# Whole float32 weights for the first token block of an attention and two-layer MLP kernel

## The chip, the cores and the metric

The kernel runs on one core of a Trainium2 chip. The metric is the device time of one execution in microseconds (us); the median of three runs of the kernel before is 1067.43 us (1066.63 to 1068.05).

## What is computed

```python
scores = scale * np.matmul(q, k.transpose(0, 1, 3, 2))     # q, k, v: (4, 8, 576, 64)
thresh = np.max(scores, axis=-1, keepdims=True) - tau
scores = np.where(scores >= thresh, scores, -1000000000.0)
attn = softmax(scores)
x = (attn @ v) as 2304 tokens x 512
h = x @ w_in;  x = where(h > 0, h, exp(min(h, 0)) - 1) @ w_out      # first layer, 512 -> 2048 -> 512
h = x @ w_in2; out = maximum(0.01 * h, h) @ w_out2                  # second layer
```

All inputs are float32, but the weights arrive as float64 words, which the kernel turns into float32 itself.

## The kernel before

Attention is cut into 32 groups: 8 ranges of queries (4 or 5 units of 64 queries) times 4 pairs of heads. A group loads `in` (K and Q, L417) and `v` (L419). For each unit TensorE makes the scores s (L446); VectorE moves them to ss with their extreme value (L450) and makes the threshold (L456); ScalarE cuts (L461) and takes the exponential (L464); VectorE inverts the sum (L467); GpSimd multiplies e by it (L469). The result has to be turned. In the first four groups TensorE turns it against an identity matrix into the PSUM tile y (L484), and two copies a unit (512 and 128 columns, L313 on ScalarE or L314 on VectorE) bring it to p. In the others VectorE transposes 32x32 blocks into t (L489), and 16 DMAs a group (L539, 13 from SP and 3 from GpSimd) exchange the blocks to p. Then TensorE multiplies p by v (L553) and a copy writes x.

Beside attention run seven blocks of 256 tokens of the first layer, each over the first 8 of 16 slices f of the hidden dimension (L591: h = x @ w_in slice; L603 to L610: g; L634: y += g @ w_out slice). To reach float32 accuracy at the rate of the reduced type fp32r, each operand is split into a rounded part (xh, wih, gh) and the rest (xl, wil, gl), and each product is three passes: high by high, low by high, high by low (`passes`, L575). The 16 tiles of weights (8 slices, wi and wo) go through `weight` (L316): DMA to wraw (L321), the high words scaled to wa (L327), the low words shifted to wb (L331, L333), two merges with two operands on VectorE (L338, L341), then rounding to wih or woh (L306, L308, L309) and a subtraction for wil or wol (L302, L303). From about 428 us attention is over, and the rest of the first layer and the second run in blocks of 512 tokens.

The order on every engine is not written out. `Order.run` (L114) is a planner: each operation has engines it may run on, a cost, what it depends on and a due time `vt`; the planner walks a modelled clock and on each engine takes the ready operation that is due first. The numbers in `KN`, the costs (`POOLI`, `LAND`, `ISSUE` and so on) and the letters that name the allowed engines (`ka='A'`: ScalarE) set the order, which is then fixed in each engine's queue. SP's queue too is in order: a DMA whose buffer is not free keeps back the ones behind it.

Of the kernel before, what the change touches and what calls it, by code (L numbers as in the profile page):

```python
# [38 lines left out]
POOLI = 1000  # L39
# [8 lines left out]
    pad=18, stay=2646.41, late=1.3, margin=0, look=0.00348273, warm=3, tu=2231.35, lead=15280.3, wv0=-1642.63,  # L48
    wv1=-1629.68, early=2925.04, boff=18361.1, bdt=7113.64, yoff=1471.44, coff=-454.38, wb=140.292, w2a=2637.92,
    o1=-3645.43, o2=1772.81, o3=4927.53, o4=-3359.29, o5=4040.73, o6=-25.7749, mo=4440.99, ka='A', kl='PA', kh='AD',  # L50
    ko='D', kt='D', kx='AD', kxl='DP', km='DP', kg='PA', kgl='P', kgl1='D', kd='DP', kc='AD', kn='P', kv='A')
# [178 lines left out]
LAND = 2100.0  # L230
ISSUE = 450
# [25 lines left out]
def attn_moe_kernel(ctx, tc, kqv, tau, w1i, w1o, w2i, w2o, yp, out):  # L257
# [21 lines left out]
    wb_r = ring(stg, 1, [128, 512], F32, "wb_")  # L279
# [36 lines left out]
    def weight(layer, which, f, vt, after=(), reg=False):  # L316
        raw, a, b = raw_r.new(), wa_r.new(), wb_r.new()
        hi, lo = wdst[which, f, "h"].new(), wdst[which, f, "l"].new()
# [24 lines left out]
            op0=ALU.bitwise_and, op1=ALU.bitwise_or), PORT), [ob], [raw, b], vt)  # L343
        oh = op(hi_of(KN["kh"], 512, hi, b), [ob], [b, hi], vt)
# [60 lines left out]
    ld = op(sp(128, 4, lambda: nc.sync.dma_start(out=taut, in_=tau.partition_broadcast(128))), [], [], -9e5)  # L405
# [4 lines left out]
    def group(gi, p, vts):  # L410
# [9 lines left out]
            out=v().rearrange("p h c d -> p (h c d)"), in_=kqv[gi * NE + p][:, KQV - 10 * D:KQV])), [], [v], due + 8e3)  # L420
# [14 lines left out]
        def units(js, vt):  # L435
# [56 lines left out]
            elif gi < GP:  # L492
                for z in range(m):
# [7 lines left out]
                    copies(lambda t=t: t()[:, 0], t, o, 0, 4, z)  # L501
                    copies(lambda t=t: t()[:, 1, 0:128], t, o, 4, 5, z)
# [26 lines left out]
    def values(gi, p, n, w, vt, by_pe, turned, tg, pg, v, lv, blocks):  # L529
        b, u0, u1 = GROUPS[gi]  # L530
        got = turned
        if not by_pe:
            got = []
            for z, (a, d) in enumerate((a, (a + r) % 4) for r in range(4) for a in range(4)):
# [6 lines left out]
                if z * NG // 16 != (z + 1) * NG // 16:  # L541
                    got.append(op((POOL, POOLI, lambda copy=copy: copy(nc.gpsimd)), turned, [pg, tg], vt + KN["o4"],
                                  lat=2500))
                else:
                    got.append(op(sp(32, 20 * w, lambda copy=copy: copy(nc.sync), 620), turned, [pg, tg],
                                  vt + KN["o4"]))
# [33 lines left out]
    def step_h(layer, f, tb, xc, hps, vt, reg):  # L580
# [14 lines left out]
        for k in range(KC):  # L595
            o = op((PE, 3 * mm(tb), lambda k=k: mms(k)), [o, wi[2], xc[k][2]],
                   [hg, wi[0], wi[1], xc[k][0], xc[k][1]], vt)
# [4 lines left out]
        if layer == 0:  # L602
# [21 lines left out]
    def step_y(layer, f, first, last, tb, g, ybank, ysl, vt):  # L624

        wo = wt[layer, "wo", f]
        res = []
        for m in range(KC):
            yg, share, end = ybank[m]

            def mms(m=m, yg=yg, share=share, end=end):
                cs = slice(m * 128, (m + 1) * 128)
                for z, (w_, g_) in enumerate(passes(wo, g)):
# [4 lines left out]
            res.append(op((PE, 3 * mm(tb), mms), [wo[2], g[2], g[3], *prev],  # L638
                          [yg, wo[0], wo[1], g[0], g[1]], vt))
# [4 lines left out]
    def block(layer, t0, fs, tb, deps, hps, yrings, evac, vt0, dt, reg=False):  # L644
        xc = conv_x(t0, tb, deps, vt0 - dt + (KN["coff"] if reg else 0), reg)
# [184 lines left out]
```

## Time and profile before

| | |
|---|---|
| median of 3 runs | 1067.43 us (1066.63 to 1068.05) |
| the profiled execution: own time, span | 1070.21 us, 1068.4 us |
| TensorE matmuls (PE) busy | 1019.3 us, 95% |
| VectorE (DVE), ScalarE (ACT), GpSimd (POOL) busy | 596.1, 508.2, 264.4 us |
| mean granted TensorE clock | 0.977 |
| DMA traffic | 120.15 MB |

The profile is one execution. Busy time of TensorE counts overlapping matmuls once; the duration of one matmul includes its way through the array, so what a matmul costs in a row of them is the distance of two starts. "PEclk" is the granted clock in parts of full speed. A releaser in brackets is what ended the idle time before an instruction. SPq is SP's queue of DMA issues.

### The profile page before, as it was taken

The page shows a single profiled execution, that of the slowest core. Times are in us where ns is not written, and L with a number is a line of the kernel's source. Part 1 is how long each engine was busy: PE and PEld are TensorE (multiplying, and loading weights), DVE is VectorE, ACT ScalarE, POOL GpSimd, SP SyncE. Part 2 cuts the span into 40 slices and gives each one's busy share as a digit, 9 for nine tenths or more (in the row PEclk, how much of TensorE's full clock was granted, in tenths as well). Part 3 has the DMA queues.
Part 4 walks back from the last instruction along what each step waited for, and adds up shares of the span by engine and source line. Part 5 has one row for each costly group of instructions (what it writes and reads, how often), then busy time and mean ns, then how long its engine had stood idle before and what let it go on. Part 6 is the DMA issues. An engine that isn't in the chain of part 4 may idle for free.

```text
span 1068.4 us, 17123 instructions
## 1 busy us (share of the span) xinstructions
PE 1019.3 (95%) x6294; PEld 807.7 (76%) x6294; DVE 596.1 (56%) x1228; ACT 508.2 (48%) x1027; POOL 264.4 (25%) x411
## 2 busy tenths in 40 slices
PE   7868899998999999999999999999999999999998
PEld 3435667776777777788888889888888888888898
DVE  6797767876777773898986547851311311221221
ACT  6887766767667673554563225532222221222221
POOL 4555655666556564101000000000000000000000
PEclk7878999999999999999999999999999999999999
DMA  6466777778777766435443003310100100010010
GB/s 207 154 181 200 203 198 201 208 210 216 189 214 193 220 184 166 140 118 187 149 124 131 28 13 99 120 60 1 40 0 1 40 1 1 1 40 1 1 40 21
DMA packets 48564, 120.15 MB, mean 112 GB/s; under 512 B 9888, under 2 KB 14496, under 8 KB 48480
## 3 DMA queue, kind: packets, MB, share of 16 engines
q1 hardware_dynamic: 45792, 111.18, 35.8%
q0 software_dynamic: 2688, 7.87, 2.7%
q8 instruction: 50, 0.82, 0.3%
q14 instruction: 34, 0.28, 0.1%
HBM read 67.63 MB, written 9.44 MB: 72 GB/s over the span
## 4 chain that ended last, share of the span: by engine, by line
PE 81%; DMA 6%; SPq 4%; DVE 3%; ACT 2%; issue 2%; POOL 0%; POOLq 0%; ACTq 0%; DVEq 0%
PE y L634 35%; PE h L591 20%; PE hb L591 15%; PE v L553 7%; PE s L446 5%; SPq L539 3%; DMA p<-t 2%; DMA in<-in_kqv_dram 2%; DMA wraw<-in_w1o_dram 1%; DVE t L489 1%; DVE ss L450 1%; PE y L484 1%; DMA wraw<-in_w1i_dram 0%; ACT e L464 0%; ACT p L313 0%
## 5 line engine op out<-in xcount | busy, mean ns | idle before, releaser
L634 PE MATMUL y<-gh,woh 128*128 128x512 f32 (+1 forms) x736 | 255.4, 347 | 2.2 <-ACT ysx L313 1.4
L634 PE MATMUL y<-gl,woh 128*128 128x512 f32 (+1 forms) x736 | 252.0, 342 | 0.0
L634 PE MATMUL y<-gh,wol 128*128 128x512 f32 (+1 forms) x736 | 251.7, 342 | 0.0
L302 DVE TENSOR_TENSOR gl<-g,gh 128x512 fp32r<-128x512 f32 (+1 forms) x128 | 83.6, 654 | 273.2 <-ACT g L617 263.4
L591 PE MATMUL h<-xh,wih 128*128 128x256 f32 (+1 forms) x480 | 163.7, 341 | 15.8 <-ACT g L603 7.2
L634 PEld LDWEIGHTS y<-gh,woh 128*128 128x128 f32 x736 | 138.9, 189 | 31.9 <-issue 10.7
L591 PE MATMUL h<-xl,wih 128*128 128x256 f32 (+1 forms) x480 | 158.2, 330 | 0.5 <-DVE xl L302 0.2
L591 PE MATMUL h<-xh,wil 128*128 128x256 f32 (+1 forms) x480 | 157.7, 329 | 0.0
L634 PEld LDWEIGHTS y<-gl,woh 128*128 128x128 f32 x736 | 139.0, 189 | 16.1
L634 PEld LDWEIGHTS y<-gh,wol 128*128 128x128 f32 x736 | 138.8, 189 | 16.2
L450 DVE TENSOR_SCALAR_CACHE_REDUCE ss<-s,scl 128x576 f32<-128x576 f32 x144 | 114.5, 799 | 31.7 <-PE s L446 31.5
L591 PEld LDWEIGHTS h<-xh,wih 128*128 128x128 f32 x480 | 90.9, 189 | 43.6 <-issue 10.4
L469 POOL TENSOR_SCALAR e<-e,su 128x576 f32<-128x576 f32 x144 | 110.2, 776 | 40.5 <-DVE su L467 35.3
L461 ACT ACTIVATE ss<-ss,thr 128x576 f32<-128x576 f32 x144 | 105.3, 769 | 16.8 <-DVE thr L456 16.4
L464 ACT ACTIVATE e<-ss,taun 128x577 f32<-128x577 f32 x144 | 110.8, 771 | 1.1 <-DVE t L489 0.4
L489 DVE STREAM_TRANSPOSE t<-e 128x640 f32<-128x640 f32 x128 | 102.2, 825 | 13.8 <-POOL e L469 7.1
L446 PE MATMUL s<-in 64*64 64x288 f32 x1152 | 95.5, 443 | 11.3 <-DVE ss L450 7.0
L553 PE MATMUL v<-p,v 128*64 128x320 f32 (+1 forms) x640 | 98.0, 439 | 7.3 <-DMA p<-t 4.3
L591 PEld LDWEIGHTS h<-xl,wih 128*128 128x128 f32 x480 | 91.0, 190 | 9.5 <-DVE xl L302 0.9
L591 PEld LDWEIGHTS h<-xh,wil 128*128 128x128 f32 x480 | 91.1, 190 | 8.2
L591 PE MATMUL hb<-xh,wih 128*128 128x512 f32 (+1 forms) x256 | 94.5, 369 | 0.0
L591 PE MATMUL hb<-xl,wih 128*128 128x512 f32 (+1 forms) x256 | 94.5, 369 | 0.0
(438 smaller groups left out, 1218.4 us busy)
## 6 DMA issues: line engine op xcount, KB each, us to landing
p<-t SPq DMA_DIRECT2D x208, 100.0 KB, 3.1
p<-t SPq DMA_DIRECT2D x156, 80.0 KB, 3.3
v<-in_kqv_dram SPq DMA_DIRECT2D x32, 320.0 KB, 3.9
in<-in_kqv_dram SPq DMA_DIRECT2D x16, 608.0 KB, 4.5
in<-in_kqv_dram SPq DMA_DIRECT2D x16, 544.0 KB, 4.3
wraw<-in_w1i_dram SPq DMA_DIRECT2D x16, 512.0 KB, 3.8
wraw<-in_w1o_dram SPq DMA_DIRECT2D x16, 512.0 KB, 3.7
wraw<-in_w2i_dram SPq DMA_DIRECT2D x16, 512.0 KB, 3.5
```

The costliest lines, as they stand in the source:

```text
L302: return pick(who, D=(dve(n), lambda: nc.vector.tensor_tensor(**args()), PORT), P=(pool_tt(n), lambda: nc.gpsimd.tensor_tensor(**args())))
L446: nc.tensor.matmul(s[z]()[64 * h:64 * h + 64, i, 0:HALF], q()[r, at:at + 64], k()[r, h], start=True, stop=True)
L450: om = [op((DVE, dve(S) + 160, lambda z=z: nc.vector.tensor_scalar(out=ss[z]()[:, 0:S].rearrange("p (j c) -> p j c", j=2), in0=s[z]()[:, : ...
L461: o = op((ACT, act(S) + 95, lambda z=z: nc.scalar.activation(out=ss[z]()[:, 0:S], in_=ss[z]()[:, 0:S], func=AF.Prelu, bias=thr()[:, z:z + ...
L464: oe.append(op((ACT, act(S) + 190, lambda z=z: nc.scalar.activation(out=e[z]()[:, 0:S + 1], in_=ss[z]()[:, 0:S + 1], func=AF.Exp, bias=tau ...
L469: on = [op(pick(KN["kn"], P=(pool_ts(S) + 90, lambda z=z: nc.gpsimd.tensor_scalar(out=e[z]()[:, 0:S], in0=e[z]()[:, 0:S], scalar1=su()[:, ...
L484: nc.tensor.transpose(dst, e[z]()[:, c * 128:(c + 1) * 128], ident)
L489: turned.append(op((DVE, dve(SX) + 70, lambda z=z, cols=cols: nc.vector.transpose(out=blocks(tg).rearrange("p d c q -> p c d q")[:, :, :, ...
L539: q.dma_start(out=to[0]()[to[1], to[2]], in_=fr[0]()[fr[1], fr[2]])
L553: nc.tensor.matmul(ps()[64 * h:64 * h + 64, 0:64 * n], v()[:, h, c, :], blocks(pg)[:, 2 * h:2 * h + 2, c], start=(c == 0), stop=(c == 4))
L591: nc.tensor.matmul(hp(), w_()[:, cs], x_()[:, 0:tb], start=(k == 0 and z == 0), stop=(k == KC - 1 and z == 2))
L634: nc.tensor.matmul(ysl(yg, m), w_()[:, cs], g_()[:, 0:tb], start=(first and z == 0 and share == 0), stop=(last and z == 2 and end))
```

## The change

For the first block of 256 tokens (`NATIVE = 1`) the kernel multiplies the merged float32 weights, x and g as they are: `step_h` and `step_y` issue one float32 matmul where three split passes stood, `conv_x` is left out, and g needs no rounding and no subtraction. The merged weights live in 17 slots of their own, so that they stay until block 0 is done; `split_w` makes the high and low parts for the later blocks with due times of their own, the low part being written into a slot whose float32 weight is no longer used. The two copies from y to p become one of 640 columns. Tau's load, the loads of v, and block 0 get due times of their own; costs in the planner and most numbers in `KN` differ, and with them the engines allowed (wa to GpSimd, x copies to VectorE, rounding of weights to GpSimd or ScalarE).

```diff
-POOLI = 1000
+POOLI = 520
+SPI = 690
+NATIVE = 1
...
-    pad=18, stay=2646.41, late=1.3, margin=0, look=0.00348273, warm=3, tu=2231.35, lead=15280.3, wv0=-1642.63,
...
-    ko='D', kt='D', kx='AD', kxl='DP', km='DP', kg='PA', kgl='P', kgl1='D', kd='DP', kc='AD', kn='P', kv='A')
+    pad=18, stay=1957.74, late=1.3, margin=0, look=0.00348273, warm=2, tu=1933.47, lead=15925.1, wv0=975.379,
...
+    o4=-3200.93, o5=4767.88, o6=-29.7579, mo=-5087.01, ka='P', kl='PA', kh='PA', ko='D', kt='D', kx='A', kxl='DP',
+    km='DP', kg='A', kgl='DP', kgl1='D', kd='P', kc='AD', kn='P', kv='D')
...
-LAND = 2100.0
-ISSUE = 450
+LAND = 2500.0
+ISSUE = 500
...
+    slots = [Ring(lambda dt, s=s: stg.tile([128, 512], dt, tag=f"w{s}", name=f"w{s}"), 1) for s in range(2 * FH + 1)]
...
+        n = 2 * f + (which == "wo")
+        raw, a, b = raw_r.new(), wa_r.new(), slots[n if reg else 2 * FH - 1].new(F32)
...
+        wt[layer, which, f] = (b, ob)
+        if not (reg and NATIVE):
+            split_w(layer, which, f, vt, reg)
+
+    def split_w(layer, which, f, vt, reg):
+        b, ob = wt[layer, which, f]
+        n = 2 * f + (which == "wo")
+        hi = wdst[which, f, "h"].new()
+        lo = slots[(n - 1) % (2 * FH + 1)].new(F32R) if f < FH else wdst[which, f, "l"].new()
...
-    ld = op(sp(128, 4, lambda: nc.sync.dma_start(out=taut, in_=tau.partition_broadcast(128))), [], [], -9e5)
+    ld = op(sp(128, 4, lambda: nc.sync.dma_start(out=taut, in_=tau.partition_broadcast(128))), [], [], KN["tl"])
...
-            out=v().rearrange("p h c d -> p (h c d)"), in_=kqv[gi * NE + p][:, KQV - 10 * D:KQV])), [], [v], due + 8e3)
+            out=v().rearrange("p h c d -> p (h c d)"), in_=kqv[gi * NE + p][:, KQV - 10 * D:KQV])), [], [v], due + KN["vl"])
...
-                    copies(lambda t=t: t()[:, 0], t, o, 0, 4, z)
-                    copies(lambda t=t: t()[:, 1, 0:128], t, o, 4, 5, z)
+                    copies(lambda t=t: t().rearrange("p b c -> p (b c)")[:, 0:640], t, o, 0, 5, z)
...
+            if whole:
+                nc.tensor.matmul(hp(), wi[0]()[:, cs], xc[k][1], start=(k == 0), stop=(k == KC - 1))
+                return
...
+                o = op((PE, mm32(tb), lambda k=k: mms(k), True), [o, wi[1], *xc[k][2]], [hg, wi[0]], vt)
...
+            d = gh if whole else g
...
+            if whole:
+                return gh, None, o, o
...
+                    nc.tensor.matmul(ysl(yg, m), wo[0]()[:, cs], g[0]().bitcast(F32)[:, 0:tb],
+                                     start=(first and share == 0), stop=(last and end))
...
+        if reg and t0 < NATIVE * TA:
+            xc = [(None, x[:, k, t0:t0 + tb], deps[k]) for k in range(KC)]
...
+        if i == NATIVE - 1:
+            for f in range(FH):
+                for j, which in enumerate(("wi", "wo")):
+                    split_w(0, which, f, need * TU + KN["wp0"] + (2 * f + j) * KN["wp1"], True)
```

How the order moves, at three places. TensorE, from the fourth value group (v<-p,v) on, before; wih and wil are the parts of the first weight slice, xh and xl those of a quarter of x:

```order
L553 MATMUL v<-p,v 64x256 x10
L446 MATMUL s<-in 64x288 x8
L591 MATMUL h<-xh_731,wih_171 128x256
L591 MATMUL h<-xl_743,wih_171 128x256
L591 MATMUL h<-xh_731,wil_176 128x256
L591 MATMUL h<-xh_368,wih_290 128x256
```

and now, w being a whole weight tile:

```order
L564 MATMUL v<-p,v 64x256 x10
L603 MATMUL h<-x,w_144 128x256
L603 MATMUL h<-x,w_232 128x256
L458 MATMUL s<-in 64x288 x8
L603 MATMUL h<-x,w_232 128x256 x3
L458 MATMUL s<-in 64x288 x12
L603 MATMUL h<-x,w_326 128x256 x4
L656 MATMUL y<-gh,w_197 128x256 x4
```

One row stands where three stood; the place beside the value groups is much the same. GpSimd, its first rows of work on weights and e, before:

```order
L331 TENSOR_SCALAR wb__149<-wraw 128x512
L303 TENSOR_TENSOR wil_176<-wb__149,wih_171 128x512
L331 TENSOR_SCALAR wb__184<-wraw 128x512
L469 TENSOR_SCALAR e_89<-e_89,su 128x576
L469 TENSOR_SCALAR e_90<-e_90,su 128x576
L303 TENSOR_TENSOR wol_246<-wb__184,woh_232 128x512
```

and now:

```order
L328 TENSOR_SCALAR wa__146<-wraw 128x512
L309 TENSOR_SCALAR wih_170<-w_144 128x512
L306 TENSOR_TENSOR w_175<-w_144,wih_170 128x512
L328 TENSOR_SCALAR wa__183<-wraw 128x512
L481 TENSOR_SCALAR e_89<-e_89,su 128x576
L481 TENSOR_SCALAR e_90<-e_90,su 128x576
L309 TENSOR_SCALAR woh_219<-w_197 128x512
```

GpSimd makes wa, which ScalarE made, and rounds weights, which VectorE or ScalarE did; w_175 is a low part. SP, in the middle of attention, before (t_87 and t_88 are the turned groups, `in` and v the loads of later groups):

```order
L539 DMA p<-t_88 32x800 x9
L419 DMA v<-in_kqv_dram 128x640
L539 DMA p<-t_88 32x800 x4
L417 DMA in<-in_kqv_dram 128x1088
L539 DMA p<-t_87 32x640 x8
L419 DMA v<-in_kqv_dram 128x640
L539 DMA p<-t_87 32x640 x5
```

and now:

```order
L550 DMA p<-t_88 32x800 x13
L429 DMA in<-in_kqv_dram 128x1088
L431 DMA v<-in_kqv_dram 128x640
L550 DMA p<-t_87 32x640 x13
L429 DMA in<-in_kqv_dram 128x1088
L431 DMA v<-in_kqv_dram 128x640
```

The load of v stands behind all 13 copies of a group where it stood among them.

## Rows read from the trace of the kernel before

**Rows 1.** Busy by stage: PE, PEld, DVE, ACT, POOL, PEclk, DMA, GB/s
```profile
0.00:145.00 145.00, 114.11 (x854) 70.08 (x856) 110.08 (x257) 107.97 (x227) 76.78 (x110) 0.85 0.63 189
145.00:425.00 280.00, 267.49 (x2359) 199.32 (x2357) 200.78 (x484) 190.01 (x418) 167.03 (x271) 0.99 0.75 200
425.00:1069.00 644.00, 637.73 (x3085) 538.34 (x3081) 285.21 (x489) 210.22 (x382) 20.61 (x30) 1.00 0.18 57
```

**Rows 2.** Chain of waits, 0 to 145 us, shares by line
```profile
by line: PE v L553 15.9%; DMA wraw<-in_w1o_dram 8.8%; issue 7.7%; PE s L446 6.9%; DMA p<-t 6.3%; SPq L539 5.8%; PE y L484 3.7%; DVE t L489 3.2%; PE h L591 2.8%; ACT e L464 2.8%; DVE ss L450 2.6%; ACT p L313 2.2%; DVE wil L302 1.5%; POOL e L
```

**Rows 3.** Groups of instructions, ScalarE, 0 to 145 us: busy us, mean ns
```profile
L313 ACT COPY p<-y 128x128 f32<-128x128 f32 (+1 forms) x20 | 7.4, 409 | 2.4 <-DVE p L314 2.4
L313 ACT COPY x<-v 128x256 f32<-128x256 f32 (+1 forms) x8 | 3.2, 395 | 10.5 <-PE v L553 10.5
L308 ACT ACTIVATE gh<-g 128x256 fp32r<-128x256 f32 x7 | 2.8, 404 | 1.6 <-DVE g L610 1.6
L333 ACT ACTIVATE wb__365<-wraw,lowb 128x512 uint32<-128x512 uint32 x1 | 0.8, 777 | 0.0
L327 ACT ACTIVATE wa__328<-wraw 128x512 f32<-128x512 f32 x1 | 0.7, 670 | 0.0
```

**Rows 4.** The same view, VectorE
```profile
L314 DVE COPY p<-y 128x512 f32<-128x512 f32 (+1 forms) x12 | 6.0, 521 | 6.8 <-PE y L484 5.4 <-ACT p L313 1.4
...
L302 DVE TENSOR_TENSOR wil<-wb__258,wih 128x512 fp32r<-128x512 f32 x1 | 0.7, 693 | 0.4 <-ACT wih L308 0.4
...
L309 DVE TENSOR_SCALAR wih<-wb__365 128x512 fp32r<-128x512 f32 x1 | 0.4, 412 | 0.0
```

**Rows 5.** The same view, GpSimd
```profile
L303 POOL TENSOR_TENSOR gl<-g,gh 128x256 fp32r<-128x256 f32 x9 | 7.6, 850 | 0.4 <-ACT gh L308 0.2
...
L303 POOL TENSOR_TENSOR wil<-wb__365,wih 128x512 fp32r<-128x512 f32 x1 | 1.3, 1274 | 2.4 <-DVE su L467 2.4
...
L331 POOL TENSOR_SCALAR wb__149<-wraw 128x512 uint32<-128x512 uint32 x1 | 0.7, 659 | 6.7 <-DMA wraw<-in_w1i_dram 6.7
```

**Rows 6.** TensorE: chain at 183 us; timeline (start, us) at 80, 144; the page's warm-up group
```profile
183.33 2.80 PE y L634 x24
...
79.99 0.41 PE L591 MATMUL h<-xl,wih 128*128 128x256 f32 x1
80.20 0.41 PE L591 MATMUL h<-xh,wil 128*128 128x256 f32 x1
...
144.12 2.38 PE L553 MATMUL v<-p,v 128*64 128x256 f32 x20
...
L393 PE MATMUL v<-ss 128*128 128x512 f32 x6 | 4.8, 958 | 1.6 <-DVE ss L387 1.6
```

**Rows 7.** Timeline of SP's queue at the start: start us, us
```profile
0.74 0.40 SPq L405 DMA_DIRECT2D taut<-in_tau_dram  x1
1.20 0.42 SPq L417 DMA_DIRECT2D in<-in_kqv_dram  x1
```

**Rows 8.** SP's waits, 145 to 425 us; chain; busy by stage; DMA issues (us to landing)
```profile
SPq L419 <- PE v L553: 19.8, 10, 4.2
...
247.94 5.04 DMA in<-in_kqv_dram
...
240.00:280.00 40.00, 36.15 (x321) 26.25 (x317) 26.50 (x68) 28.51 (x63) 22.88 (x38) 0.96 0.80 212
...
p<-t SPq DMA_DIRECT2D x208, 100.0 KB, 3.1
...
v<-in_kqv_dram SPq DMA_DIRECT2D x32, 320.0 KB, 3.9
```

**Rows 9.** Timeline of TensorE behind the last value group
```profile
428.16 0.50 PE L591 MATMUL h<-xh,wih 128*128 128x512 f32 x1 [1.35 <-ACT xh L308]
```

**Rows 10.** Timeline of VectorE and GpSimd at 71 us
```profile
70.96 2.21 DVE L302 TENSOR_TENSOR wil<-wb__738,wih 128x512 fp32r<-128x512 f32 x1 [0.35 <-ACT wih L308]
...
71.16 1.46 POOL L469 TENSOR_SCALAR e<-e,su 128x576 f32<-128x576 f32 x2
```

More of the change, by code (lines that the diff above doesn't have):

```diff
@@ L544, in values @@
                 else:
-                    got.append(op(sp(32, 20 * w, lambda copy=copy: copy(nc.sync), 620), turned, [pg, tg],
+                    got.append(op(sp(32, 20 * w, lambda copy=copy: copy(nc.sync), SPI), turned, [pg, tg],
                                   vt + KN["o4"]))
@@ L586, in step_h @@
         wi = wt[layer, "wi", f]
+        whole = xc[0][0] is None
         def mms(k):
             cs = slice(k * 128, (k + 1) * 128)
+            if whole:
+                nc.tensor.matmul(hp(), wi[0]()[:, cs], xc[k][1], start=(k == 0), stop=(k == KC - 1))
+                return
             for z, (w_, x_) in enumerate(passes(wi, xc[k])):
@@ L595, in step_h @@
         for k in range(KC):
[L596 to L597 removed]
+            if whole:
+                o = op((PE, mm32(tb), lambda k=k: mms(k), True), [o, wi[1], *xc[k][2]], [hg, wi[0]], vt)
+            else:
+                o = op((PE, 3 * mm(tb), lambda k=k: mms(k)), [o, wi[2], xc[k][2]],
+                       [hg, wi[0], wi[1], xc[k][0], xc[k][1]], vt)
         lasth[0] = o
@@ L609, in step_h @@
                    [o], [g], vt)
+            d = gh if whole else g
             o = op((DVE, dve(tb), lambda: nc.vector.scalar_tensor_tensor(
-                out=g()[:, cs], in0=g()[:, cs], scalar=0.0, in1=hp(), op0=ALU.min, op1=ALU.max)),
-                [o], [hg, g], vt)
+                out=d().bitcast(F32)[:, cs], in0=g()[:, cs], scalar=0.0, in1=hp(), op0=ALU.min, op1=ALU.max)),
+                [o], [hg, g, d], vt)
+            if whole:
+                return gh, None, o, o
             o1 = op(hi_of(KN["kg"] if reg else "A", tb, lambda: gh()[:, cs], lambda: g()[:, cs]), [o], [g, gh], vt)
@@ L626, in step_y @@
         wo = wt[layer, "wo", f]
+        whole = g[1] is None
         res = []
@@ L632, in mms @@
                 cs = slice(m * 128, (m + 1) * 128)
+                if whole:
+                    nc.tensor.matmul(ysl(yg, m), wo[0]()[:, cs], g[0]().bitcast(F32)[:, 0:tb],
+                                     start=(first and share == 0), stop=(last and end))
+                    return
                 for z, (w_, g_) in enumerate(passes(wo, g)):
@@ L637, in step_y @@
             prev = [res[m - 1]] if share else []
-            res.append(op((PE, 3 * mm(tb), mms), [wo[2], g[2], g[3], *prev],
-                          [yg, wo[0], wo[1], g[0], g[1]], vt))
+            if whole:
+                res.append(op((PE, mm32(tb), mms, True), [wo[1], g[2], *prev], [yg, wo[0], g[0]], vt))
+            else:
+                res.append(op((PE, 3 * mm(tb), mms), [wo[2], g[2], g[3], *prev],
+                              [yg, wo[0], wo[1], g[0], g[1]], vt))
         return res
```

13 lines of the change are left out of this document (6 added, 7 removed).

## Prediction

> **What bounds the kernel now.** I read the stages first, then the chain of waits in the first of them, then the costs of single instructions. The busy times by stage [rows 1] are to show three programs. From 425 us to the end TensorE is busy 637.73 of 644 us: nothing but TensorE counts there. From 145 to 425 us it is busy 267.49 of 280 us, so 12.5 us are idle. Up to 145 us it is busy 114.11 us at a mean granted clock of 0.85, VectorE 110.08 and ScalarE 107.97: three engines at about three quarters each, none full. The chain of that stage [rows 2] is to show the same: TensorE's lines (15.9% + 6.9% + 3.7% + 2.8%) make some 30% of it, and the rest hops between landing weights, the SP queue, ScalarE, VectorE and GpSimd. So the first 145 us (48 units of attention and the 16 weight tiles) are where instructions off ScalarE and VectorE are worth time. The sum below is against this execution (span 1068.4, own time 1070.21 us), which lies 2.78 above the median of the runs, 1067.43.
>
> **The pace of the first stage.** From the two orders I count what each engine does up to the 48th unit. ScalarE: 16 multiplications to wa leave it (0.67 each) and 2 more low-word conversions come (0.78); 20 copies to p (7.4 us) become 11 of 640 elements (about 0.68 each, a little over the 512-element copy); 9 copies to x go (0.395); 8 roundings of g and x go (0.404) [rows 3]. That is -10.7 + 1.6 + 0.1 - 3.6 - 3.2 = -15.8. VectorE: 7 roundings of weights go (0.41) and 6 subtractions (0.69), 12 copies to p (6.0 us) become 5 of about 0.82, and 9 copies to x come to it, about 0.45 each, a little under the mean of its copies to p (0.52) [rows 4]: -2.9 - 4.1 - 1.9 + 4.1 = -4.8. GpSimd: 16 multiplications to wa and 8 weight roundings come (about the 0.66 of its low-word conversion) and two such conversions go, 5 weight subtractions come (1.27), 9 subtractions for gl go (0.85) [rows 5]: +10.6 + 5.3 - 1.3 + 6.4 - 7.7 = +13.3. A few smaller instructions on each about cancel. GpSimd thus goes from 76.78 to 90 us of 145, ScalarE to 92, VectorE to 105.3. VectorE stays the fullest: at its present fill of 110.08 in 145 us this takes 138.7 us, **-6.3 us**. I take that value, since the stage can't run ahead of the engine left on top. One end is 0 (loads and TensorE keep the chain as long as it is); the other is the relief of both engines lying in one path, 20.6 of their 218 us, or -13.7.
>
> **Native passes.** 64 groups of three split passes (32 for h, 32 for y) become one float32 matmul each. Split passes cost 2.80/24 = 0.117 us each back to back, so 0.35 for three, and 0.21 each, 0.63 for three, about 80 us, where the lower clock is granted [rows 6]. A float32 matmul shows as two records. Ten over 256 columns, five pairs side by side, take 2.38 us, 0.48 a pair; the six records over 512 columns at the start are busy 4.8 us, 0.8 each, and as long for two of 256 columns. The first pair of prices is the nearer one (the same width, in the stage's own work): about 0.46 against 0.35, so 64 x 0.106 = 6.8 us of TensorE work more. TensorE idles 31 us in this stage and is 30% of its chain, so I charge 30%: **+2.0 us**. Ends: 0, and +9.1 if all of it is exposed and a third at the doubled price of the lower clock (a mean of 0.85 is about that share). The Trainium skill's page FP8 and Floating Point Precision (TensorE Precision Notes) speaks against the change: true float32 is four passes through the array, where the split has three. By that, 64 x 0.117 = 7.5 us would be added, an estimate, and the charge would be 2.2 instead of 2.0; the trace's pair of matmuls agrees with it.
>
> **First loads.** The first load of `in` is issued ahead of tau's instead of behind it, at 0.74 instead of 1.20 us [rows 7], and the first scores wait for it: **-0.5 us**. Of the three warm-up matmuls one goes; the wait for the load covers them either way. Tau comes half a microsecond later, under the first scores.
>
> **The middle.** By the ninth value group TensorE has done 216 passes of the blocks beside attention before, and 64 native matmuls (worth 192) with 36 passes now. So 12 passes fewer are left, 12 x 0.117 = **-1.4 us**; all other TensorE work there is the same. On the SP queue a load of v stood among the 13 copies to p and waited there for value matmuls: 19.8 us in ten waits, with copies and the next load of `in` queued behind it [rows 8]. Now it stands after all 13 copies, and the load of `in` mostly right ahead of it. One landing of `in` that the chain went through took 5.04 us at 248 us; around it and the next one TensorE idles 3.85 us of 40 and is granted 0.96 of its clock, 1.6 us more. I take half of the 5.4, **-2.7**, since `in` still stands behind 13 copies. Ends: -12.5, all idle time of the stage; and a loss where v is now the later one: in nine groups (19 and 24 to 31) its load follows its own group's copies, and lands 0.4 + 3.9 - 3.1 = 1.2 us behind them [rows 7, 8], +11 in all if no other work covers it.
>
> The split of the 16 weights for later blocks is in the counts above, mostly on GpSimd. If its cover fails, the first h of block 1 is late next, since each low part is written over a float32 tile that block 0 must have done with. At the end of attention the wait of 1.35 us for the rounding of x [rows 9] goes, since y passes of the last block now stand between the first h passes of 512 columns: **-1.3**. From there TensorE's order is the same; weight work on the other engines is paced a little otherwise, under a TensorE that is never idle: 0.
>
> **Sum:** -6.3 + 2.0 - 0.5 - 1.4 - 2.7 - 1.3 = -10.2. The profiled execution would take 1060.0, the median 1057.2 us.
>
> **Rivals.** (a) *TensorE is the bound of the first stage.* Place: block 0, 60 to 130 us. The 114 busy us get 9.1 more (the upper end above) and the relief of the others buys nothing, there or in the middle, where TensorE is 95% busy: 1067.4 + 9.1 - 0.5 = 1076. It decides once TensorE is some 95% busy in that stretch. For it speaks the low clock, which doubles each added pass; against it, that TensorE is 79% busy now and 70% of the chain lies elsewhere. Chance 0.13.
> (b) *VectorE and GpSimd hold each other up.* At 70.96 us a subtraction on VectorE took 2.21 us, not the 0.69 of rows 4, over two GpSimd multiplications that began 0.2 us after it [rows 10]. The 32 weight merges with two operands in SBUF stay on VectorE, and GpSimd gets 27 weight instructions more beside them. If each of 16 tiles meets a hold of 0.7 us, VectorE gets 11 us back: 1068. It decides by how often they meet; against it, the other merges of the first stage hardly show it. Chance 0.13. The Trainium skill, SBUF — State Buffer (SBUF: two separate sides), has this as a rule: a VectorE instruction with two SBUF inputs and a GpSimd one that reads SBUF exclude each other for a whole instruction. By that rule VectorE's relief would be given back, as in (b).
> (c) *The SP queue set the pace of the middle.* Then its whole 12.5 us go in place of 1.4 + 2.7 + 1.3, and 1067.4 - 6.3 + 2.0 - 0.5 - 12.5 = 1050; with the other end of the first stage, 1043. For it: the waits of rows 8; against it: TensorE at 95%. Chance 0.14.
> That the change doesn't do what it says is out: the order shows 64 native matmuls and no split pass of block 0.
>
> **How the numbers follow.** Forecast 0.60, (a) 0.13, (b) 0.13, (c) 0.14. A measurement of this kernel can tell about 0.2%, or 2.1 us, from no change. (b) spreads about no change: half of it is within 0.2%, a quarter on either side. The forecast's own range is 1051 to 1064, from half of the relief lost to half of the other end won. Faster: 0.60 + 0.14 + 0.03 = 0.77; same 0.07; slower 0.13 + 0.03 = 0.16. The range takes in (b) up to 1069 and most of (c) down to 1045, and leaves out (a) and the tails.
>
> **What would show it.** Right: the 48th reduction ends near 138 us instead of 144.8; ScalarE is some 16 us less busy up to there and VectorE the fullest; native matmuls take about 0.46 us and TensorE still idles beside them; no load of v waits inside a run of copies; TensorE idles some 10 us in the middle; the time from the handover to the end is unchanged. Wrong: native matmuls of 0.8 us with TensorE full (a); merges well above 0.69 us (b); a first stage as long as before; or value matmuls of groups 24 to 31 that wait for v.

## The result

The changed kernel takes 1052.67 us (median of 4 runs, 1050.85 to 1055.2), the kernel before 1067.03 in the runs beside it. The ratio is 0.9869 with an interval of 0.9844 to 0.9895: some 14 us faster, where 10 were forecast. The profiled execution has a span of 1049.1 us (own time 1050.85); it lies 1.8 below its median and that of before 3.2 above (1070.21 against 1067.03), so the two profiles differ by 19.3 us of span, about 5 more than the kernels do.

Busy time by stage after, the view of [rows 1] (us; PE, PEld, DVE, ACT, POOL, granted clock, DMA share, GB/s):

```profile
0.00:145.00 145.00, 122.62 (x942) 75.49 (x943) 117.88 (x273) 106.04 (x214) 101.87 (x143) 0.94 0.70 208
145.00:425.00 280.00, 264.42 (x2281) 193.88 (x2280) 217.75 (x501) 183.47 (x404) 151.35 (x238) 1.00 0.73 200
425.00:1069.00 644.00, 620.46 (x3008) 525.31 (x3006) 263.97 (x422) 207.85 (x375) 54.19 (x62) 1.00 0.16 53
```

In the first 145 us every engine but ScalarE does more than before: the stage got denser and reaches further in the work. So a fixed window compares unlike work, and I cut at a piece of work instead: the end of the 48th reduction of scores (L450 before, L462 after). That is the first stage by content. The same view, cut there, before:

```profile
0.00:144.80 144.80, 113.91 (x852) 69.93 (x854) 109.91 (x255) 107.97 (x227) 76.76 (x110) 0.85 0.63 189
```

and after:

```profile
0.00:127.80 127.80, 106.06 (x792) 62.92 (x792) 103.12 (x238) 94.20 (x186) 92.50 (x128) 0.93 0.69 204
```

The stage is **17.0 us shorter**. VectorE is busy 6.8 us less, and not busy 24.7 us instead of 34.9, which is the other 10.2. The chain of waits of the first 145 us, answering to [rows 2], now has more of TensorE (6.0% and 9.3% at L603 and L656, the native passes, that is the single float32 matmuls) and less of landing weights, 4.7% where 8.8% stood:

```profile
by line: PE v L564 11.4%; PE y L656 9.3%; PE s L458 9.2%; DMA p<-t 7.3%; issue 7.3%; PE h L603 6.0%; DMA wraw<-in_w1i_dram 4.7%; SPq L550 4.7%; ACT ss L473 4.4%; ACT e L476 4.4%; DVE ss L462 4.3%; PE h L606 3.5%; POOL e L481 2.4%; PE y L496
```

What VectorE waited for up to the 48th reduction (us in total, times, longest), before:

```profile
DVE ss L450 <- PE s L446: 6.7, 4, 3.2
DVE p L314 <- PE y L484: 5.4, 6, 1.8
DVE t L489 <- DMA p<-t: 3.6, 2, 3.4
DVE su L467 <- ACT e L464: 3.0, 4, 1.4
DVE g L610 <- PE h L591: 2.8, 2, 2.1
DVE taup L398 <- DMA taut<-in_tau_dram: 2.1, 1, 2.1
```

and after:

```profile
DVE taup L410 <- DMA taut<-in_tau_dram: 4.8, 1, 4.8
DVE x L317 <- PE v L564: 3.5, 5, 1.2
DVE w L341 <- ACT w L336: 2.9, 3, 2.1
DVE w L341 <- POOL wa__794 L328: 2.9, 1, 2.9
DVE t L501 <- DMA p<-t: 2.2, 3, 1.2
DVE gh L629 <- PE h L603: 1.8, 2, 1.5
DVE su L479 <- ACT e L476: 1.2, 3, 0.6
DVE t L501 <- POOL e L481: 1.1, 2, 0.7
DVE ss L462 <- PE s L458: 0.9, 3, 0.4
```

The waits for scores and for turned tiles, 12.1 us before, are 0.9 plus a single one of 0.5. Of the 12.1, 2.8 stood before the very first reduction, where VectorE now waits for tau instead, 4.8 us for 2.1. For the rest, TensorE's scores and turned tiles now lie ready when VectorE comes for them.

Behind the first stage little changed. The first h pass of 512 columns, the handover of [rows 9], starts 281.5 us behind the 48th reduction (283.4 before), and from it to the end are 639.8 us (640.2):

```profile
409.29 0.50 PE L606 MATMUL h<-xh,wih 128*128 128x512 f32 x1 [0.72 <-ACT xh L311]
```

So of 19.3 us in the profiles, 17.0 come from the first stage, 1.9 from the middle with the handover, 0.4 from the rest.

### The profile page after: what moved, and what is told of

Read it like the earlier page. It is cut to its first block, busy times and chain, and to the rows that moved or that the text cites. A ratio compares the mean times of both kernels' runs of the same rounds, so it can differ in the third digit from the quotient of the medians.

```text
span 1049.1 us, 17092 instructions
## 1 busy us (share of the span) xinstructions
PE 1007.5 (96%) x6228; PEld 794.7 (76%) x6228; DVE 599.6 (57%) x1194; ACT 497.4 (47%) x991; POOL 307.4 (29%) x441
## 4 chain that ended last, share of the span: by engine, by line
PE 81%; DMA 5%; DVE 5%; ACT 4%; issue 2%; SPq 2%; POOL 1%; DVEq 0%; ACTq 0%; POOLq 0%
PE y L660 35%; PE h L606 20%; PE hb L606 15%; PE v L564 5%; PE s L458 4%; DMA p<-t 3%; SPq L550 2%; DMA in<-in_kqv_dram 2%; PE y L656 1%; ACT e L476 1%; DVE t L501 1%; DVE ss L462 1%; ACT ss L473 1%; PE h L603 1%; DVE thr L468 1%
## 5 line engine op out<-in xcount | busy, mean ns | idle before, releaser
L660 PE MATMUL y<-gh,woh 128*128 128x512 f32 (+1 forms) x704 | 245.8, 349 | 2.8 <-ACT ysx L316 2.0
L305 DVE TENSOR_TENSOR gl<-g,gh 128x512 fp32r<-128x512 f32 (+1 forms) x143 | 91.6, 641 | 271.4 <-ACT g L638 257.7
L660 PE MATMUL y<-gl,woh 128*128 128x512 f32 (+1 forms) x704 | 242.7, 345 | 0.0
L606 PE MATMUL h<-xh,wih 128*128 128x256 f32 (+1 forms) x448 | 153.2, 342 | 9.3 <-DVE g L629 4.6
L606 PE MATMUL h<-xl,wih 128*128 128x256 f32 (+1 forms) x448 | 148.4, 331 | 0.3 <-DVE xl L305 0.3
L481 POOL TENSOR_SCALAR e<-e,su 128x576 f32<-128x576 f32 x144 | 114.5, 805 | 39.9 <-DVE su L479 35.1
L660 PE MATMUL y<-gh,w 128*128 128x256 f32 (+1 forms) x384 | 124.9, 325 | 0.0
L660 PE MATMUL y<-gh,wol 128*128 128x512 f32 (+1 forms) x320 | 117.7, 368 | 0.0
L462 DVE TENSOR_SCALAR_CACHE_REDUCE ss<-s,scl 128x576 f32<-128x576 f32 x144 | 113.3, 797 | 3.7 <-PE s L458 3.4
L501 DVE STREAM_TRANSPOSE t<-e 128x640 f32<-128x640 f32 x128 | 102.0, 824 | 11.4 <-POOL e L481 5.6
L564 PE MATMUL v<-p,v 128*64 128x320 f32 (+1 forms) x640 | 87.0, 411 | 6.5 <-DMA p<-t 3.3
L606 PE MATMUL h<-xh,w 128*128 128x256 f32 (+1 forms) x288 | 89.2, 310 | 0.0
L636 ACT ACTIVATE gh<-h 128x512 fp32r<-128x512 f32 (+1 forms) x40 | 22.2, 555 | 137.5 <-PE h L606 137.5
```

What stands on the lines that cost most here:

```text
L305: return pick(who, D=(dve(n), lambda: nc.vector.tensor_tensor(**args()), PORT), P=(pool_tt(n), lambda: nc.gpsimd.tensor_tensor(**args())))
L462: om = [op((DVE, dve(S) + 160, lambda z=z: nc.vector.tensor_scalar(out=ss[z]()[:, 0:S].rearrange("p (j c) -> p j c", j=2), in0=s[z]()[:, : ...
L481: on = [op(pick(KN["kn"], P=(pool_ts(S) + 90, lambda z=z: nc.gpsimd.tensor_scalar(out=e[z]()[:, 0:S], in0=e[z]()[:, 0:S], scalar1=su()[:, ...
L501: turned.append(op((DVE, dve(SX) + 70, lambda z=z, cols=cols: nc.vector.transpose(out=blocks(tg).rearrange("p d c q -> p c d q")[:, :, :, ...
L564: nc.tensor.matmul(ps()[64 * h:64 * h + 64, 0:64 * n], v()[:, h, c, :], blocks(pg)[:, 2 * h:2 * h + 2, c], start=(c == 0), stop=(c == 4))
L606: nc.tensor.matmul(hp(), w_()[:, cs], x_()[:, 0:tb], start=(k == 0 and z == 0), stop=(k == KC - 1 and z == 2))
```

## The experiments

Three cuts describe every run: the end of the 48th reduction, with VectorE's busy and other time up to there; the first h pass of 512 columns; the end of the span. All are of one profiled execution each, in us; the ratio is that of the medians to before.

| kernel | 48th ends | VectorE busy + not | from there to 512 columns | to the end | ratio, interval |
|---|---|---|---|---|---|
| before | 144.8 | 109.9 + 34.9 | 283.4 | 640.2 | |
| the change | 127.8 | 103.1 + 24.7 | 281.5 | 639.8 | 0.9869 [0.9844, 0.9895] |
| a_split | 136.6 | 114.5 + 22.1 | 289.0 | 643.0 | 1.0067 [1.0044, 1.0090] |
| v_native | 130.3 | 101.9 + 28.4 | 303.9 | 640.3 | 1.0081 [1.0050, 1.0113] |
| b_native | 140.2 | 107.4 + 32.8 | 284.1 | 640.2 | 0.9993 [0.9974, 1.0012] |
| b_all | 138.1 | 109.6 + 28.5 | 287.2 | 641.0 | 1.0005 [0.9981, 1.0029] |
| b_vdup | 148.9 | 121.4 + 27.5 | 283.5 | 640.2 | 1.0053 [1.0038, 1.0068] |
| a_double | 152.6 | 104.2 + 48.4 | 283.1 | 640.1 | 1.0100 [1.0069, 1.0131] |
| a_half | 126.6 | 102.9 + 23.7 | 281.1 | 639.9 | 0.9848 [0.9801, 0.9895] |
| a_vdup | 141.7 | 116.8 + 24.9 | 282.2 | 640.1 | 0.9976 [0.9953, 0.9999] |
| a_switch | 131.3 | 103.6 + 27.7 | 284.1 | 639.8 | 0.9903 [0.9869, 0.9936] |
| a_pool | 129.4 | 104.0 + 25.4 | 284.2 | 644.6 | 0.9931 [0.9908, 0.9954] |
| h_letters | 136.9 | 110.0 + 26.9 | 298.0 | 643.2 | 1.0117 [1.0100, 1.0134] |
| h_block | 137.3 | 102.6 + 34.7 | 288.1 | 642.8 | 1.0023 [1.0011, 1.0035] |

### Which part brings the gain

**a_split**: the change with split passes again in block 0, planned anew.

```diff
-NATIVE = 1
+NATIVE = 0
```

> The changed kernel with NATIVE = 0: block 0 is split into three passes as the other blocks, weights are split where they land; all other numbers and engines of the change stay, and the planner orders it anew. Theory (relief of ScalarE and VectorE by moves to GpSimd and merged copies sets the pace of the first stage, the native passes only help by taking splits away): about half of the 14 us stays, 1058 to 1062 us, with the 48th reduction near 135 us. Rival 1 (whole weights are the cause, since block 0 no longer waits for split weights): 1065 us or more, 48th reduction at 142 us or later. Rival 2 (the new due times of the planner are the cause, native or not): 1055 us or less.

Measured 1073.45 us. Up to the 48th reduction:

```profile
0.00:136.60 136.60, 107.43 (x847) 65.68 (x847) 114.47 (x246) 98.06 (x198) 97.07 (x131) 0.89 0.65 189
```

VectorE is busy 11.4 us more than in the change, not busy 2.6 less, and the stage is 8.8 longer. Then 7.5 us more go between there and the first 512 columns, and 3.2 behind. With these numbers the native passes are worth 20.8 us (some 15 against two other plans of the change, below), and in the first stage they act through VectorE.

**v_native**: the change with all numbers, letters and costs of before (block 0's pace, the loads of v and tau's due as before had them; the due times of the later splits stay), planned anew.

```diff
-POOLI = 520
-SPI = 690
+POOLI = 1000
+SPI = 620
...
-LAND = 2500.0
-ISSUE = 500
+LAND = 2100.0
+ISSUE = 450
```

> The changed kernel's code with NATIVE = 1, but with the planner's numbers, costs and engine letters of the kernel before (wa on ScalarE, roundings on VectorE and ScalarE); the order is planned anew. Theory: ScalarE keeps wa (16 x 0.67 us), so only part is gained, 1058 to 1063 us. Rival 1 (whole weights are the cause): 1055 us or less. Rival 2 (the due times are the cause): 1065 us or more.

Measured 1076.14 us. The first stage is nearly as good as in the change, 130.3 us:

```profile
0.00:130.30 130.30, 104.30 (x765) 60.78 (x766) 101.94 (x241) 96.40 (x195) 72.88 (x105) 0.90 0.67 200
```

But the middle takes 303.9 us, 22.4 more, in which TensorE is busy 281.03: this plan leaves 22.8 us idle, of which the waits for p alone are 9.4.

```profile
130.30:434.10 303.80, 281.03 (x2395) 205.46 (x2394) 202.98 (x500) 191.99 (x423) 168.02 (x269) 0.99 0.72 191
```

```profile
PE v L564 <- DMA p<-t: 9.4, 7, 2.2
```

Part of its short first stage is work put off: TensorE shows 765 records up to the 48th reduction where the change shows 792. And VectorE still waits for scores:

```profile
DVE ss L462 <- PE s L458: 9.8, 6, 3.6
```

**b_native**: the kernel before in its own order on every engine, with native matmuls in block 0 and the rounding and subtraction of x and g left out there; the weights are split where they were, and their rounded part is the operand.

```diff
+            if whole:
+                nc.tensor.matmul(hp(), wi[0]().bitcast(F32)[:, cs], x[:, k, 0:tb], start=(k == 0), stop=(k == KC - 1))
+                return
...
```

> The kernel before, every engine's order kept word for word, but block 0 takes whole float32 operands: the 192 split passes become 64 float32 matmuls and the 8 instructions that split x and the 16 that split g go. The weight operand is the rounded part, so that nothing else moves (the product then lacks the weights' low part, and its time is the same). Theory: TensorE work grows by 64 x 0.08 = 5 us with 30% exposed, and 24 small instructions go: -2 to +2 us against the kernel before. Rival 1 (native passes by themselves are the gain): -8 us or more.

Measured 1066.6 us, no change that can be told (its profile has a span of 1064.5, and before's 1068.4 is of an execution 2.9 above the median of the runs beside this one). VectorE is 2.5 us less busy, and the 48th reduction ends 4.6 earlier (139.4 in the next expectation is where that reduction starts). The passes by themselves, in the old order, bring little.

**b_all**: b_native, and also wa on GpSimd, one copy of 640 elements, and loads of v behind the 13 copies, still in the order of before.

```diff
-            A=(act(512), lambda: nc.scalar.mul(out=a(), in_=top().bitcast(F32), mul=2.0 ** -112))),
+            A=(act(512), lambda: nc.gpsimd.tensor_scalar(
+                out=a(), in0=top().bitcast(F32), scalar1=2.0 ** -112, scalar2=1.0, op0=ALU.mult, op1=ALU.mult) if reg
...
-                    copies(lambda t=t: t()[:, 0], t, o, 0, 4, z)
-                    copies(lambda t=t: t()[:, 1, 0:128], t, o, 4, 5, z)
+                    copies(lambda t=t: t().rearrange("p b c -> p (b c)")[:, 0:640], t, o, 0, 5, z, 4)
...
+            if inrun[0] % 13:
+                held_v.append(fn)
```

> All changes of instructions in the order of before: native block 0 (rounding, subtraction of x and g left out there, the weights still split where they were), the wa multiplications on GpSimd, one copy of 640 elements in place of 512 and 128, loads of v behind the 13 copies. VectorE is relieved about as in the native run in that order (48th reduction there 139.4), ScalarE of 11 us more. If VectorE paces the stage and the rest of the gain lies in the order: 48th reduction at 136 to 140, in all 1062 to 1067. If the instructions bring the gain: 48th near 130, in all 1053 to 1058.

Measured 1067.77 us. Up to the 48th reduction:

```profile
0.00:138.10 138.10, 109.78 (x788) 64.43 (x790) 109.57 (x246) 96.14 (x192) 82.10 (x114) 0.91 0.65 193
```

ScalarE is 11.8 us less busy than before, nearly as much as in the change, and VectorE 2.2 us more than in b_native. The stage is 2.1 us shorter than there, and in all it brings nothing. These changes without the new order don't make the gain. They are not all of the change: the roundings of weights and the copies of x stay on their old engines here, and VectorE is 6.5 us busier than in the change.

### What the new numbers do

**h_block**: the change with the five numbers that pace the token blocks put back, planned anew.

```diff
-... boff=60357, bdt=4966.54, yoff=3469.29, coff=6893.89, ... bd0=14949
+... boff=18361.1, bdt=7113.64, yoff=1471.44, coff=-454.38, ... bd0=7113.64
```

> The changed kernel with the five numbers that pace block 0 to 2 beside attention put back (boff, bdt, bd0, yoff, coff), planned anew; letters and the numbers of attention stay. Level of no effect 1057 to 1060, from two other re-plannings. If the later and slower start of the blocks took VectorE's waits away: 1063 or more, with VectorE idle over 30 us up to the 48th reduction. If not: 1052 to 1060 and an idle of about 25 us.

Measured 1070.16 us:

```profile
0.00:137.30 137.30, 109.84 (x794) 64.69 (x796) 102.61 (x240) 94.58 (x187) 92.09 (x126) 0.91 0.68 201
```

VectorE has the busy time of the change, 102.6, and the other time of before, 34.7 against 34.9. In this plan the five numbers are worth 10 us of VectorE's waits, but these are not the waits that the change took away: those for scores and turned tiles are 2.1 us here and were 12.1. What grew over the change are waits for GpSimd, for block 0's h and for ScalarE's sums:

```profile
DVE t L501 <- POOL e L481: 4.4, 4, 2.7
DVE gh L629 <- PE h L603: 4.2, 2, 2.3
...
DVE su L479 <- ACT e L476: 3.5, 7, 0.8
...
DVE ss L462 <- PE s L458: 1.7, 2, 1.3
...
DVE p L317 <- PE y L496: 0.4, 1, 0.4
```

Nor do the five old numbers make 34.7 us by themselves: v_native has them too, and its other time is 28.4.

**h_letters**: the change with the seven letters that choose the engines put back, planned anew.

```diff
-... ka='P', ... kh='PA', ... kx='A', ... kg='A', kgl='DP', ... kd='P', ... kv='D'
+... ka='A', ... kh='AD', ... kx='AD', ... kg='PA', kgl='P', ... kd='DP', ... kv='A'
```

> The changed kernel with the seven changed letters of the table put back (which engine may take wa, the roundings of weights, x and g, the two subtractions, the copies to x), planned anew; all numbers stay. Two other re-plannings of the changed kernel lay at 1057.4 and 1060.0, so that is the level of no effect. If the letters carry the gain: 1063 or more, with VectorE busy over 106 us up to the 48th reduction. If the numbers do: 1052 to 1060.

Measured 1080.2 us:

```profile
0.00:136.90 136.90, 103.98 (x762) 58.15 (x764) 109.97 (x245) 97.30 (x196) 74.75 (x104) 0.89 0.65 198
```

The mirror image: VectorE's other time is about that of the change, 26.9, and its busy time that of before, 110.0; GpSimd has 17.8 us less. The stage is 9.1 longer. Another 16.5 go up to the first 512 columns, with TensorE idle 23.8 of 298 us:

```profile
136.90:434.90 298.00, 274.21 (x2398) 204.35 (x2394) 208.71 (x491) 190.60 (x421) 171.76 (x272) 0.99 0.69 189
```

Taken together: up to the 48th reduction VectorE's waits for scores and turned tiles come to 10.7 to 12.1 us in the five kernels with the old numbers or the old order (before, v_native, b_native, b_all, b_vdup) and to 0.5 to 3.5 in the six planned with the new numbers (the change, a_split, h_block, h_letters and the two that follow). Split passes, the old letters and the old pace of the blocks, each put back alone, do not bring these waits back. By elimination it is the other new numbers, attention's due times and the costs, that removed them; no run puts those back alone.

**a_switch, a_pool**: two plannings of the change with a number moved that has nothing to do with it.

```diff
-SWITCH = 91
+SWITCH = 92
```

> The changed kernel with one number of the planner's table moved by one (SWITCH 92 instead of 91), so that the same instructions are planned into another order; no instruction is added or left out. If the 14 us come from the instructions: within 3 us, 1050 to 1056. If they come in good part from the one order that the tuned numbers happen to give: several us worse, 1056 to 1070.

```diff
-POOLI = 520
+POOLI = 525
```

> A second re-planning of the changed kernel (the planner's price of a DMA issue on GpSimd 525 instead of 520), the same instructions in another order. As with the switch: within 3 us (1050 to 1056) if the instructions bring the gain, 1056 to 1070 if the particular order does.

Measured 1057.44 and 1059.96 us: 5 and 7 us of the change's 14 are gone, with the same instructions in another order. The first stage is 3.5 and 1.6 us longer, the middle 2.6 and 2.7; a_pool's end takes 644.6, since TensorE waits once for g behind the handover, and is granted a clock of 0.91 in the 20 us from there (1.00 in the change):

```profile
PE h L606 <- DVE g L629: 3.3, 1, 3.3
```

So a third to a half of the gain is this particular order, and the losses of h_block and h_letters count from about 1058.7, not from 1052.7.

### Which engine sets the pace

**a_double**: the change in its order, each native matmul issued twice (block 0's products enter twice).

```diff
-                nc.tensor.matmul(hp(), wi[0]()[:, cs], xc[k][1], start=(k == 0), stop=(k == KC - 1))
+                for z in range(2):
+                    nc.tensor.matmul(hp(), wi[0]()[:, cs], xc[k][1], start=(k == 0 and z == 0), stop=(k == KC - 1 and z == 1))
...
+                    for z in range(2):
...
```

> The changed kernel in its own order, each of the 64 native matmuls issued twice into the same sum (block 0 then holds twice its product). That adds 64 x 0.43 = 27.5 us of TensorE work to the first stage. Theory (TensorE is some 30% of the chain there): 8 us slower than the changed kernel, up to 12. Rival (a) of the prediction (TensorE is the bound of the stage): 25 us or more slower.

Measured 1078.54 us, 25.9 more than the change:

```profile
0.00:152.60 152.60, 132.44 (x920) 86.98 (x920) 104.16 (x238) 94.49 (x187) 91.63 (x128) 0.96 0.60 176
```

TensorE is busy 26.4 us more and the stage is 24.8 longer: 94% of the added work shows.

**a_half**: the reverse, 32 of the 64 left out (half of h's and half of y's).

```diff
-                nc.tensor.matmul(hp(), wi[0]()[:, cs], xc[k][1], start=(k == 0), stop=(k == KC - 1))
+                if k % 2 == 0:
+                    nc.tensor.matmul(hp(), wi[0]()[:, cs], xc[k][1], start=(k == 0), stop=(k == KC - 2))
...
+                    if first or last or (f + m) % 3 == 0:
...
```

> The changed kernel in its order with 32 of the 64 native matmuls left out (the odd k of each h, and 16 of the 32 of y), so block 0's results lack those parts. Removed: 32 x 0.43 = 13.8 us of TensorE work in the first stage, nothing else on any engine. TensorE is the bound at the margin there (doubling them cost 94% of what was added): some 12 to 13 us less, 1040. My charge of 30%: 4 us less, 1048.5. Left-out work opens gaps and brings the lower granted clock back: less than 12 us, with a mean granted clock of the first 127 us below 0.93.

Measured 1050.72 us, 2 less than the change, with intervals that overlap:

```profile
0.00:126.60 126.60, 97.71 (x728) 52.62 (x728) 102.86 (x238) 93.55 (x186) 91.78 (x128) 0.89 0.71 208
```

TensorE is busy 8.4 us less and the stage 1.2 us shorter. (32 matmuls of 0.43 would be 13.8 us; the granted clock fell from 0.93 to 0.89.) So TensorE does not bound the change; that reading of a_double falls. It stands close behind what does. That its lines are the largest part of the chain above (some 40%) does not show the pace.

**a_vdup**: the change in its order, VectorE's sign merge of the 16 weight tiles twice.

```diff
+        def merge():
+            for _ in range(2 if reg else 1):
+                nc.vector.scalar_tensor_tensor(
...
-        ob = op((DVE, dve(512), lambda: nc.vector.scalar_tensor_tensor(
+        ob = op((DVE, dve(512), merge, PORT), [ob], [raw, b], vt)
```

> The changed kernel in its order, with VectorE's sign merge of each of the 16 weight tiles of block 0 done twice (the second changes nothing): 16 x 0.73 = 11.7 us more on VectorE in the first stage, the mirror of the doubled matmuls. If VectorE sets the pace of the stage, as my first term had it: some 9 to 12 us more, 1062 to 1065. If TensorE does, and VectorE follows within its slack (busy 102 of the first 127 us): within 2 us of the changed kernel, 1051 to 1055.

Measured 1065.29 us, 12.6 more than the change:

```profile
0.00:141.70 141.70, 112.53 (x792) 66.52 (x792) 116.82 (x254) 94.79 (x187) 93.13 (x128) 0.89 0.63 185
```

**b_vdup**: the same in the kernel before, in its order.

```diff
+            for _ in range(2 if reg else 1):
...
-        ob = op((DVE, dve(512), lambda: nc.vector.scalar_tensor_tensor(
+        ob = op((DVE, dve(512), merge, PORT), [ob], [raw, b], vt)
```

> The kernel before in its order, with VectorE's sign merge of each of the 16 weight tiles done twice (the second changes nothing): 16 x 0.68 = 10.8 us more on VectorE up to the 48th reduction, where it was busy 109.9 of 144.8 us. If VectorE set the pace of the first stage before as well: 9 to 12 us more there (48th reduction at 153 to 156) and 8 to 12 us in all, 1075 to 1079. If the 35 us in which VectorE was not busy are slack that others set: under 4 us, below 1071.

Measured 1073.21 us, 5.6 more than before:

```profile
0.00:148.90 148.90, 114.36 (x852) 68.88 (x854) 121.42 (x271) 108.97 (x227) 76.85 (x110) 0.85 0.62 184
```

In the change, VectorE's 13.7 us more lengthen the stage by 13.9, and its other time stays (24.9 against 24.7): added work on VectorE shows in full. After a_double that alone does not prove that VectorE sets the pace, and no run takes work from it in this order. What speaks for VectorE is that taking work from TensorE brought next to nothing, and that up to the 48th reduction TensorE's longest wait in the change is for VectorE:

```profile
PE s L458 <- DVE ss L462: 7.6, 4, 3.5
```

The doubled merge also lies in the way of the weights, but up to there TensorE waits nowhere for a merged one. Before, 11.5 us more lengthened it by 4.1, and 7.4 went into waits that were there anyway: there VectorE was in the pace only in part. Neither of the two expectations for b_vdup holds; the value lies between.

## Why the prediction was right, and where its sum was off

The forecast was right in sign and near in size: 1057.2 against 1052.7, in the range. Some of that nearness is luck: the profiled executions, for which it was summed, differ by 19.3 us and not by 10.2. The three terms of the first stage come to -4.8 where -17.0 was measured, and the rest to -5.4 where -2.3 was. Nor do the range's ends follow from its words: half of 6.3 lost and half the way to -13.7 won give 1053.5 to 1060.4, and the measured time lies just below that. Its terms:

**The pace of the first stage, -6.3, was the mis-sized one: -17.0, native passes and first loads included.** The engine was right as far as the runs show (a_vdup, a_half), and the counts were close: VectorE was to lose 4.8 us of work and lost 6.8, ScalarE 15.8 and lost 13.8, GpSimd to get 13.3 and got 15.7. What failed is the step "at its present fill": that VectorE's other time shrinks only in proportion, by 1.5 us. It fell by 10.2, and the waits for scores and turned tiles alone by 10.7. They are gone in each plan with the new numbers, native or split, and still there with native passes, wa on GpSimd, merged copies and late loads of v in the old order (b_all, 10.7). So the new order took them away; which of the numbers made it so is known only by elimination, as said under h_letters. I read the new numbers in the table as a cause of the order and priced only the instructions that it moves; the view to price was the list of VectorE's waits above, where 12.1 us stood for scores and turned tiles. My end of -13.7, the whole relief of two engines, was too tight too.

**Native passes, +2.0 as 30% of 6.8.** The price was near. Eight records, four matmuls, take 1.73 us from start to start of the next line, 0.43 a matmul:

```profile
84.28 1.89 PE L603 MATMUL h<-x,w 128*128 128x256 f32 x8
86.01 0.59 PE L656 MATMUL y<-gh,w 128*128 128x256 f32 x2
```

The Trainium skill, FP8 and Floating Point Precision (TensorE Precision Notes), counts four passes, which at 0.117 would be 0.47, an estimate; the trace lies between that and the 0.35 of three. A share of 30% exists nowhere: of 8.4 us of TensorE taken away 1.2 showed, of 26.4 us added 24.8. Native matmuls were cheap here: leaving half of them out saved 2 us, with intervals that overlap.

**First loads, -0.5: nothing came.** The load of `in` goes first, but tau lands behind it, and VectorE waits for tau instead of the scores; its first reduction starts at 7.08 us, and at 7.04 before. Before, then after:

```profile
3.59 0.15 DVE L398 TENSOR_SCALAR taup<-taut 128x1 f32<-128x1 f32 x1 [2.08 <-DMA taut<-in_tau_dram]
...
7.04 0.82 DVE L450 TENSOR_SCALAR_CACHE_REDUCE ss<-s,scl 128x576 f32<-128x576 f32 x1 [2.80 <-PE s L446]
```

```profile
6.29 0.15 DVE L410 TENSOR_SCALAR taup<-taut 128x1 f32<-128x1 f32 x1 [4.78 <-DMA taut<-in_tau_dram]
...
7.08 0.82 DVE L462 TENSOR_SCALAR_CACHE_REDUCE ss<-s,scl 128x576 f32<-128x576 f32 x1
```

"Under the first scores" was wrong: tau came 2.7 us later, not half a microsecond.

**The middle and the handover, -4.1 and -1.3: -1.9 together.** SP no longer waits at a load of v inside a run of copies; from 145 to 425 us no wait of that load is left where 19.8 us were [rows 8], and none of VectorE's or TensorE's longer waits is for v. It bought nothing that shows: between the 48th reduction and the 512 columns TensorE idled 13.9 us before and 15.9 after. Its busy time there fell by 3.9, of which 1.4 were forecast. Before, then after:

```profile
144.80:428.16 283.36, 269.50 (x2372) 200.17 (x2369) 201.73 (x487) 191.12 (x421) 167.06 (x272) 0.99 0.75 200
```

```profile
127.80:409.29 281.49, 265.57 (x2368) 194.23 (x2366) 218.85 (x515) 186.91 (x418) 156.53 (x247) 1.00 0.75 206
```

SP's queue waits elsewhere instead, from 145 to 425 us for 19.0 us at loads of weights, where no such wait stood before:

```profile
SPq L324 <- DVE w L344: 19.0, 4, 5.4
```

At the handover 0.72 us of the 1.35 are left, as x is still rounded last. Here a wait in SP's queue was worth no more than what TensorE idled for it.

**The rivals.** (a) TensorE as the bound fails for this change (a_half), though it is true a little further on (a_double). (b) fails in its price: the 32 merges of the first 145 us take 13.08 + 11.65 = 24.73 us, and took 24.80 before, though GpSimd is busy 101.9 us instead of 76.8.

```profile
0.00:145.00 145.00, 13.08 (x16) 0.94 0.70 208
0.00:145.00 145.00, 11.65 (x16) 0.94 0.70 208
```

The hold itself is there. Nine of the 32 merges take over 0.72 us, and each of them ends 0.54 to 0.55 us behind a GpSimd instruction that was running when it began; 11 of GpSimd's 52 multiplications of e begin under a merge and take 1.05 to 1.24 us, where the median is 0.75. An example of each, from the timeline after: two multiplications end at 20.50 us, and the merge that began under the second of them at 21.04; and two multiplications of which the first began under a merge take 1.81 us together, not 1.47:

```profile
19.03 1.47 POOL L481 TENSOR_SCALAR e<-e,su 128x576 f32<-128x576 f32 x2 [0.19 <-DVE su L479]
...
20.13 0.91 DVE L341 SCALAR_TENSOR_TENSOR w<-wa__228,w 128x512 uint32<-128x512 uint32 x1
```

```profile
52.20 0.69 DVE L344 SCALAR_TENSOR_TENSOR w<-wraw,w 128x512 uint32<-128x512 uint32 x1
52.41 1.81 POOL L481 TENSOR_SCALAR e<-e,su 128x576 f32<-128x576 f32 x2 [2.10 <-DVE su L479]
```

The Trainium skill's rule (SBUF — State Buffer, SBUF: two separate sides) has the two exclude each other for whole instructions. The trace agrees, by the numbers above. But the one that comes second waits, and in this order GpSimd paid more often than before (11 such multiplications over 1 us instead of 2), while the merges as a whole got no longer.

(c) gives nearly the measured time by the wrong place: the middle hardly moved.

**What stays open.** Why the planned order of the change is 5 to 7 us better than its two neighbours was not taken apart further than the table shows. ScalarE and GpSimd, busy 94.2 and 92.5 of the first 127.8 us, were given no added work, and none of the three engines beside TensorE was relieved in this order, so that ScalarE or GpSimd stands as close as VectorE is possible. No neighbouring plans of the kernel before were made, so how good its order is among them is not known. That the late due times of the blocks help because attention's instructions then lie ahead of block 0's on each engine is argued, not shown. h_letters and a_split lose 16.5 and 7.5 us in the middle under plans of their own, so their totals don't measure the letters or the passes alone; their first stages do so better, though h_letters, like v_native, has put off some of TensorE's work there (762 records, not 792).

## What to carry to other kernels

Where several engines are each three quarters busy, add work to each in turn in the fixed order: what shows in full may set the pace, and taking work away shows whether it does or only stands right behind (here adding was tried with TensorE and VectorE, taking away with TensorE alone). Split a stage at a piece of work, not at a time, and price the busy time and the waits of the pacing engine separately, and do not take one from the other: with the new instructions of b_all in the old order, VectorE's busy time fell by 0.3 us and its other time by 6.4. With a planner, run one or two plans with an unrelated number moved before crediting a gain to an edit; here that scatter was a third to a half of the gain.

## What the runs showed of the hardware

TensorE's busy time in the whole program fell by 11.8 us (1019.3 to 1007.5), though the native passes are 64 x (0.43 - 0.35) = 5 us dearer. The clock is the likely reason, not shown by a run of its own: in the first stage the granted clock, a mean over its two levels of 1.2 and 2.4 GHz, went from 0.85 to 0.93: from 75 to 100 us, where it was 0.75 before, it is 1.00. Before, with TensorE busy 20.60 of 25 us, and after, with 23.32:

```profile
75.00:100.00 25.00, 20.60 (x156) 13.72 (x153) 19.57 (x45) 19.01 (x39) 13.64 (x17) 0.75 0.73 206
```

```profile
75.00:100.00 25.00, 23.32 (x166) 14.09 (x168) 20.99 (x50) 17.75 (x35) 22.18 (x29) 1.00 0.64 175
```

The higher clock does not account for VectorE's shorter waits: a_vdup, in the order of the change, has 0.89 up to the 48th reduction and the same other time (24.9), while h_block has 0.91 and an other time as before. (a_half has 0.89 too and is no slower than the change, but with half of the native matmuls gone.) No run shows the order of the change at the 0.85 of before.
